# Two token tiles at a time in the fronts of the channel groups, with the ranks found anew (DeltaNet and a low-rank mixer on one core)

## The chip, the core and the metric

One core of a Trainium2 chip. The metric is device time in microseconds (us) of one execution. Engines are named as in the profile: PE is TensorE (PEld its weight loads), DVE is VectorE, ACT is ScalarE, POOL is GpSimd, SP is SyncE, which issues transfers.

## The reference

Two blocks, all in float32. The first runs a delta-rule recurrence over 768 tokens for 4 batches and 8 heads of dimension 48; the second mixes tokens through a rank of 32 and channels through a hidden width of 1536.

```python
k_n = k / (np.linalg.norm(k, axis=-1, keepdims=True) + 1e-06)
for t in range(S):
    y[:, :, t] = einsum('bhd,bhde->bhe', q[:, :, t], state)
    v_old = einsum('bhde,bhd->bhe', state, k_n[:, :, t])
    state = state + beta[:, :, t] * einsum('bhd,bhe->bhde', k_n[:, :, t], v[:, :, t] - v_old)
x = y.transpose(0, 2, 1, 3).reshape(B, S, H * D)      # (4, 768, 384)
h = x.transpose(0, 2, 1) @ U @ V                       # U (768, 32), V (32, 768)
u = x + h.transpose(0, 2, 1)
out = u + np.maximum(u @ w_ch1, 0.0) @ w_ch2           # 384 -> 1536 -> 384
```

## The kernel before

The recurrence is done in chunks of 64 tokens. A batch has 12 chunks; six of them make a unit, so there are 8 units n, two to a batch. Units 0, 2, 4, 6 use the SBUF tile slot_87 and units 1, 3, 5, 7 slot_88, so the loads for a unit wait until the unit two before it is done.

For each unit: `load` brings k, q, v and a second copy of k (called z in the names) in pieces of 72 KB; `grams` transposes k and q on PE (L478), copies them out on ACT (L493) and makes the products of a chunk with itself (L505), which DVE masks (L518, L536); `norms` takes the norms of k from the diagonal, and scales v on DVE (L461). `blocks` inverts the triangular 32x32 blocks on DVE: a transposition into gs (L587), a scaling (L591), pairs of multiply and subtract (L596, L602), a transposition back into zz (L609); then the blocks are joined on PE (L652, L666, L692 to L713). `recur(b)` first lets PE apply the inverse (L811, L822), then goes through the 12 chunks of a batch: PE L860, DVE z (L873), PE L888, DVE s (L898, in the first chunk the copy L900), with the outputs on PE (L775, L789) and copied by ACT into X (L759).

The weights come as float64 and are taken apart and put together as float32 on DVE in five instructions a slice (L989, L995, L1001, L1007, L1017) with one on ACT (L974): U, V, six slices of w1, six of w2. SP issues their transfers (L967).

The mixer works in channel groups of 256 tokens (GT), three to a batch (i = 0, 1, 2). Each has a `front` and a `wide` part. In the front of the first group of a batch PE forms x^T U for the whole batch (L1040) and DVE copies it to tt (L1046). Then a group's two tiles of 128 tokens go through `block(c)`, one tile each: PE multiplies tt with V (L1054) into one PSUM bank, DVE adds it to x in place (L1058), PE transposes the tile in three pieces (L1062), ACT copies them into ut (L1065). `wide` waits for both tiles of the group, then PE does 36 matmuls into the hidden width (L1132), ACT the relu (L1088), DVE sums for a seven-product scheme (L1104, L1111), PE 42 matmuls back (L1169), and DVE adds the products to x (L1117); the result goes out through SP (L1121).

PSUM is split into four pairs of banks; a step that needs PSUM takes a pair, also where it uses one bank of it. Once the last chunks of batch 0 are out, one pair becomes the two banks of the mixer.

The order of all instructions is fixed when the program is built. Every part is a Python generator that yields `op(engine, cost, ...)` for each step; `run()` keeps a clock of assumed costs for each engine and picks, of the steps that can start soon, the one with the lowest rank. A rank is the second argument of `begin`, or, if the part is named in the text PLACES (L140 to L164, 91 entries), the number there. `hold` (L238) says how much later than the earliest a step with a good rank may start. The engines then run their queues in the order so found, each instruction waiting for what it needs. A change of ranks, of an assumed cost or of the engine that a step is booked on can therefore move any instruction on any queue.

In `load`, the second half of the pieces of units 2 to 7 is issued by POOL (L378), but its time is booked on SP.

Of the kernel before, what the change touches and what calls it, by code (L numbers as in the profile page):

```python
# [11 lines left out]
ALU = mybir.AluOpType  # L12
# [7 lines left out]
GT = 256  # L20
# [6 lines left out]
def kernel(  # L27
# [20 lines left out]
    nc = tc.nc  # L48
# [45 lines left out]
    def dve(n):  # L94
        return (n + 151) / 960.0

    def act(n):
        return 0.16 + n / 1200.0
# [39 lines left out]
            waits[i] = s  # L138

    PLACES = """  # L140
    add_up b1 i0 15.701; block b0 i0 c0 64.5; block b0 i1 c2 71.091; block b0 i1 c3 56.313
    block b0 i2 c5 93.473; block b1 i0 c0 14.618; block b1 i0 c1 14.618; block b1 i1 c2 14.618
    block b1 i1 c3 14.618; block b1 i2 c4 14.618; block b1 i2 c5 14.618; block b2 i0 c0 93.5
    block b2 i0 c1 93.5; block b2 i1 c2 93.5; block b2 i1 c3 93.5; block b3 i0 c0 65.835
    block b3 i0 c1 65.835; block b3 i2 c4 65.835; block b3 i2 c5 65.835; blocks n0 1.5
    blocks n3 97.0; blocks n5 79.5; diagonals n1 h0 59.5; front b1 i0 79.5
    front b2 i0 58.8; gather b0 i0 h1 c0 70.591; gather b0 i1 h1 c0 70.591; gather b0 i1 h1 c1 70.591
    gather b1 i0 h1 c1 79.0; gather b1 i2 h1 c0 97.0; gather b2 i0 h0 c0 21.0; gather b2 i1 h1 c0 21.0
    gather b2 i1 h1 c1 21.0; grams n2 i0 81.482; grams n2 i1 89.482; grams n3 i0 20.0
    grams n5 i0 31.5; grams n5 i1 20.5; grams n7 i0 13.5; joins n1 h0 12.5  # L150
    joins n2 h0 -3.0; joins n2 h1 -3.0; joins n7 h0 106.5; joins n7 h1 102.5
    last_sum b0 i0 74.5; last_sum b2 i0 27.644; load n0 namev halves(0, 1) 74.591; load n1 namek halves(0, 1) 49.32
    load n1 nameq halves(0, 1) 49.32; load n1 namez halves(0, 1) 49.82; load n4 namek halves(0, 1) 86.5; load n7 namek halves(0, 1) 75.587
    load_beta u0 14.5; load_weights 68.5; norms n1 59.3; norms n2 81.804
    norms n7 91.523; outputs b0 c2 3.5; outputs b0 c4 76.5; outputs b0 c6 46.644
    outputs b0 c7 36.586; outputs b0 c9 90.5; outputs b1 c11 9.0; outputs b1 c5 57.185
    outputs b2 c0 37.5; outputs b2 c11 37.5; outputs b2 c5 37.5; outputs b3 c5 79.0
    placed n6 i1 j0 6.5; prepare n2 h1 5.0; prepare n3 h1 37.477; products n0 i0 j1 58
    products n0 i1 j1 58; products n1 i0 j0 81.119; products n2 i0 j1 3.5; products n2 i1 j0 76.0
    products n3 i0 j0 66.5; products n3 i0 j1 21.301; products n4 i1 j0 58.0; products n5 i1 j0 79.5  # L160
    products n5 i1 j1 79.5; products n6 i1 j0 53.243; products n6 i1 j1 70.0; products n7 i1 j0 87.58
    recur b2 46.313; recur b3 72.5; relu b0 i1 60.403; relu b1 i2 23.537
    wide b0 i0 81.619; wide b0 i1 92.619; wide b2 i1 103
    """  # L164
    PLACES = dict(x.strip().rsplit(" ", 1) for x in PLACES.replace("\n", ";").split(";") if x.strip())

# [42 lines left out]
    def run():  # L209
        stall = {}  # L210
        while waits or woken:
            while woken:
                i = woken.pop(0)
                at = max([0.0] + [done[x] for x in asked[i]])
                if at > ready[i]:
                    last[i] = None
                advance(i, None, max(at, ready[i]))
            some = {}
            for i, s in waits.items():
                e, was = s["e"], last.get(i)  # L220
                at = max(was[1] if was and was[0] == e else ready[i], clock[e])
                if s["port"]:
                    at = max(at, clock["port"])
                if s["take"]:
                    banks, of = places(s)
                    if not of:
                        continue
                    at = max(at, min(banks[y] for y in of))
                if s["mode"] and s["mode"] != state["mode"]:
                    at += SWITCH  # L230
                stall[i] = late(s, at)[1]
                some.setdefault(e, []).append((at + stall[i], i))
            picks = []
            for e, them in some.items():
                soon = min(at for at, _ in them)
                them.sort(key=lambda x: (not waits[x[1]]["rush"], x[1]))
                for at, i in them:
                    hold = 0.5 if i[0] < 13 else HOLD if i[0] < 90 else SWITCH  # L238
                    if at > soon + hold:
                        continue  # L240
                    if not any(a < at and a + waits[x]["cost"] < at + 0.05 for a, x in them):
                        picks.append((at, i))
                        break
            at, i = min(picks)
            at -= stall[i]
            s, got = waits[i], None
            if s["take"]:
                banks, of = places(s)
                got = min(of, key=lambda y: (banks[y], y))
                del banks[got]  # L250
            if s["e"] == "pe":
                pace(at, at, 0.0)
            cost = cost_of(s)
            if s["e"] == "pe":
                crossed, more = late(s, at)
                state["lot"] += s["words"]
                if state["lot"] > LOT:
                    state["lot"] -= LOT
                    cost += more
                    behind = max(0.0, state["hw"] - crossed - more - 0.5)  # L260
                    state["fetched"] = crossed + more + FETCH + 0.6 * behind
                pace(at, at + cost, s["flow"])
            state["now"] = clock[s["e"]] = at + cost
            if s["port"]:
                clock["port"] = at + cost
            if s["mode"]:
                state["mode"] = s["mode"]
            for tag, x in s["give"]:
                free[tag][x] = state["now"] + s["lat"]
            last[i] = s["e"], state["now"]  # L270
            advance(i, got, state["now"] + s["lat"])
# [4 lines left out]
    def one(x):  # L276
        return P[:, BANK["pair"][x]]
# [86 lines left out]
    def load(n, name, halves):  # L364
# [7 lines left out]
            e = "sp" if halves == (0,) else "act"  # L372
        else:
            e = "sp"
        queue = dict(sp=nc.sync, act=nc.scalar)[e]
        for g in halves:
            if n >= NU and g:
                queue = nc.gpsimd  # L378
            for s in range(1, 4, 2) if name == "z" else range(4):
                to = dict(k=s, q=s, v=s % 2 * 2 + s // 2, z=s // 2)[name]  # L380
                yield op(e, 0.65, port=False)
                queue.dma_start(  # L382
                    out=t[half(1 - g if name == "z" else g), :, to, 0:D],
                    in_=src[b, 4 * g + s, hf * UC * L : (hf + 1) * UC * L, :].rearrange(
                        "(c t) d -> t c d", t=L
                    ),
                )
                after = landing(384)
                if name == "z" or s % 2:
                    emitted((name, n, g, s // 2), after)  # L390
# [165 lines left out]
    def halves(t, split):  # L556

        size = BK // split
        flat = t.rearrange("p a b -> p (a b)")[:, 0 : split * size * (BK + (split > 1))]
        return flat.rearrange("p (u x) -> p u x", u=split)[:, :, 0 : size * BK].rearrange(  # L560
            "p u (a b) -> p u a b", b=BK
        )[:, :, :, 0:size]
# [467 lines left out]
    def front(b, i):  # L1030
# [17 lines left out]
        cs = list(range(i * GT // 128, (i + 1) * GT // 128))  # L1048
        ut = uts[b, i] = mix.tile([128, KT, GT], FP32, name="ut")

        def block(c):
            o = yield op("pe", 0.65, "F", take="pair", words=4)
            p_h = one(o)[:, 0:DM]
            nc.tensor.matmul(  # L1054
                p_h, v_sb[:, c * 128 : (c + 1) * 128], tt, start=True, stop=True
            )
            yield op("dve", dve(384), give=[("pair", o)])
            nc.vector.tensor_tensor(out=x[:, c], in0=x[:, c], in1=p_h, op=ALU.add)  # L1058
            o = yield op("pe", 0.56, "F", take="pair", words=6, flow=0.32)
            p_u = one(o)[:, 0:DM].rearrange("p (t n) -> p t n", t=KT)  # L1060
            for t in range(KT):
                nc.tensor.transpose(p_u[:, t], x[:, c, t * 128 : (t + 1) * 128], ident)  # L1062
            at = c * 128 - i * GT
            yield op("act", act(384), give=[("pair", o)])
            nc.scalar.copy(ut[:, :, at : at + 128], p_u)  # L1065
            emitted(("ut", b, c))

        for c in cs:
            begin(block(c), 2)
        yield need(*[("ut", b, c) for c in cs])  # L1070
        emitted(("front", b, i), 0.1)

    def reserve():
# [157 lines left out]
```

## Time and profile before

| | |
|---|---|
| median of 3 runs | 622.55 us (621.05 to 623.77) |
| the profiled execution's own time | 622.19 us |
| its span, first to last instruction | 620.1 us |
| mean granted PE clock | 0.939 |
| PE busy | 0 to 124 us: 100.1; 124 to 620 us: 489.0 |
| L1132, 864 records | 201.9 us, 385 ns each |
| L1169, 1008 records | 176.1 us, 329 ns each |
| DVE, L596 and L602 | 64.1 and 64.6 us |
| DMA moved | 33.26 MB |

The span is what the profile can divide up; the time of the execution is 2.1 us longer than its span. Granted clock is the share of full TensorE speed that PE was given in a stretch. A float32 matmul shows as two records, a transposition as one. Busy time of an engine is the union of its instructions, so durations of neighbours that overlap add to a little more.

### The profile page before, as it was taken

Reading aid. Unit: us, or ns where it says so; the run is one execution under the profiler, and the core shown is the slowest. Engines: PE = TensorE matmul, PEld = TensorE weight load, DVE = VectorE, ACT = ScalarE, POOL = GpSimd, SP = SyncE. Lnnn points to the kernel's source line nnn. Section 1 sums busy time; section 2 is a strip of 40 time slices with the busy share of each in tenths; the row PEclk is TensorE's granted clock in tenths of the full one; section 3 lists DMA queues with packets and bytes.
Section 4 is the critical chain, followed back from the end, with each engine's and each line's share of the span. In section 5 each row is a group of like instructions: output and inputs, shape, how many; then the busy total and the mean of one; then the engine's idle time right before and its main releaser. Section 6 shows DMA issues by size and latency. Waiting matters only on the chain.

```text
span 620.1 us, 23438 instructions
## 1 busy us (share of the span) xinstructions
PE 589.1 (95%) x10536; PEld 518.6 (84%) x10536; DVE 401.0 (65%) x965; ACT 228.3 (37%) x450; POOL 82.5 (13%) x145
## 2 busy tenths in 40 slices
PE   6678988999999999999999999999999999999997
PEld 5578976789888878799889878889889869898987
DVE  5869997898989613889898128898894123131312
ACT  3465564740342553521621643245324321101020
POOL 3011052410010343200100511401001000000000
PEclk9766565999999999999999999999999999999999
DMA  9840568850000332410000611600000000000000
GB/s 146 159 88 5 177 177 177 186 123 14 15 4 29 64 75 52 77 37 0 30 3 13 113 41 30 133 2 3 30 3 14 16 3 9 18 5 21 15 12 25
DMA packets 72004, 33.26 MB, mean 54 GB/s; under 512 B 59616, under 2 KB 70368, under 8 KB 71904
## 3 DMA queue, kind: packets, MB, share of 16 engines
q1 hardware_dynamic: 66112, 24.98, 18.3%
q0 software_dynamic: 4192, 6.49, 4.6%
q8 instruction: 82, 1.34, 0.9%
q10 hardware_dynamic: 1600, 0.30, 0.3%
q14 instruction: 18, 0.15, 0.1%
HBM read 27.03 MB, written 4.72 MB: 51 GB/s over the span
## 4 chain that ended last, share of the span: by engine, by line
PE 82%; DVE 9%; SPq 5%; issue 2%; DMA 1%; ACT 0%; ACTq 0%; DVEq 0%
PE P L1132 30%; PE P L1169 27%; SPq L382 4%; PE P L505 3%; PE P L478 2%; PE P L860 2%; PE P L1054 2%; PE P L775 2%; PE P L888 2%; PE P L811 2%; PE P L789 2%; DVE prod L596 1%; DVE xt L602 1%; PE P L822 1%; PE P L666 1%
## 5 line engine op out<-in xcount | busy, mean ns | idle before, releaser
L1132 PE MATMUL P<-ut,w_sb 128*128 128x256 f32 x864 | 201.9, 385 | 0.0
L1132 PEld LDWEIGHTS P<-ut,w_sb 128*128 128x128 f32 x864 | 159.4, 190 | 22.4 <-issue 0.6
L1169 PE MATMUL P<-w_sb,hs 128*128 128x192 f32 x720 | 125.6, 329 | 0.0
L1169 PEld LDWEIGHTS P<-w_sb,hs 128*128 128x128 f32 x720 | 117.1, 190 | 3.9 <-issue 1.2
L1088 ACT ACTIVATE hs<-P 128x512 f32<-128x512 f32 x72 | 43.0, 597 | 167.1 <-PE P L1132 163.1
L1117 DVE TENSOR_TENSOR X<-X,P 128x192 f32<-128x192 f32 x84 | 29.4, 350 | 62.7 <-PE P L1169 62.1
L602 DVE TENSOR_TENSOR xt<-xt,prod 128x112 f32<-128x112 f32 (+21 forms) x200 | 64.6, 323 | 6.9
L596 DVE TENSOR_TENSOR prod<-gs,xt 128x112 f32<-128x112 f32 (+21 forms) x200 | 64.1, 321 | 4.8
L759 ACT COPY X<-P 64x192 f32<-64x192 f32 x96 | 30.1, 313 | 71.3 <-PE P L789 54.6
L1169 PE MATMUL P<-w_sb,S 128*128 128x192 f32 x288 | 50.5, 329 | 0.0
L1169 PEld LDWEIGHTS P<-w_sb,S 128*128 128x128 f32 x288 | 46.8, 190 | 0.6
L1104 DVE TENSOR_TENSOR S<-hs 128x384 f32<-128x384 f32 x24 | 13.2, 552 | 52.4 <-ACT hs L1088 52.3
L873 DVE TENSOR_TENSOR z<-slot,P 128x192 f32<-128x192 f32 x44 | 15.5, 352 | 45.6 <-PE P L860 30.8
L478 PE MATMUL P<-ident,slot 128*128 128x128 f32 x192 | 30.4, 309 | 13.4 <-DMA slot<-in_k_dram 11.4
L478 PEld LDWEIGHTS P<-ident,slot 128*128 128x128 f32 x192 | 25.0, 158 | 18.3 <-issue 13.2
L731 ACT COPY slot<-zz 32x384 f32<-32x384 f32 x64 | 32.5, 509 | 12.2 <-DVE zz L609 7.9
L493 ACT COPY slot<-P 128x768 f32<-128x768 f32 x30 | 23.7, 803 | 31.1 <-PE P L478 30.9
L581 POOL MEMSET xt<- 128x1056 f32 x8 | 7.8, 980 | 186.7 <-DVE zz L609 186.7
L505 PE MATMUL P<-slot 48*64 48x64 f32 x1536 | 31.8, 238 | 0.5 <-ACT slot L493 0.2
L505 PEld LDWEIGHTS P<-slot 48*64 48x64 f32 x1536 | 28.7, 150 | 3.9 <-ACT slot L493 2.1
L738 POOL MEMSET slot<- 32x384 f32 x32 | 13.6, 424 | 108.6 <-PE P L695 63.0
L382 POOL DMA_DIRECT2D slot<-in_k_dram x36 | 24.2, 679 | 28.1 <-PE P L888 28.1
(119 smaller groups left out, 780.7 us busy)
## 6 DMA issues: line engine op xcount, KB each, us to landing
out_dram<-X SPq DMA_DIRECT2D x24, 192.0 KB, 1.9
slot<-in_k_dram SPq DMA_DIRECT2D x56, 72.0 KB, 4.0
X<-in_moe_w_ch_dram SPq DMA_DIRECT2D x10, 384.0 KB, 5.5
wide<-in_moe_w_ch_dram SPq DMA_DIRECT2D x10, 384.0 KB, 5.1
slot<-in_q_dram SPq DMA_DIRECT2D x40, 72.0 KB, 3.6
slot<-in_v_dram SPq DMA_DIRECT2D x40, 72.0 KB, 2.7
slot<-in_k_dram POOLq DMA_DIRECT2D x36, 72.0 KB, 3.9
slot<-in_q_dram POOLq DMA_DIRECT2D x24, 72.0 KB, 4.6
```

The lines of the kernel that those rows point to most:

```text
L382: queue.dma_start(out=t[half(1 - g if name == "z" else g), :, to, 0:D], in_=src[b, 4 * g + s, hf * UC * L : (hf + 1) * UC * L, :].rearrang ...
L478: nc.tensor.transpose(p_t[:, c // 3, c % 3], t[:, c, 2 * j : 2 * j + 2].rearrange("p s d -> p (s d)"), ident,)
L493: nc.scalar.copy(to, p_t)
L505: nc.tensor.matmul(p_g[half(g ^ (par * i)), par, c], kq[rows, c, j, 0, half(g)], kq[rows, c, j, i, half(g)], start=True, stop=True,)
L596: nc.vector.tensor_tensor(out=prod, in0=gb[:, :, j : j + 1, j + 1 :].to_broadcast([128, split, m, w]), in1=xb[:, :, 0:m, j : j + 1].to_bro ...
L602: nc.vector.tensor_tensor(out=xb[:, :, 0:m, j + 1 :], in0=xb[:, :, 0:m, j + 1 :], in1=prod, op=ALU.subtract,)
L731: nc.scalar.copy(pg[quarter(i), :, at, :, a : a + BK], cut(zc, h)[quarter(i)].rearrange("p r (c j) t -> p r c j t", j=2),)
L759: nc.scalar.copy(x[half(c % 2), c // 2, 4 * D * g : 4 * D * (g + 1)].rearrange("p (j r d) -> p r j d", r=2, d=D), states(p_y)[half(g)],)
L1088: nc.scalar.activation(hs[:, fs[0] : fs[1] + 1 : fs[1] - fs[0]], p_f, ACTF.Relu)
L1117: nc.vector.tensor_tensor(out=to, in0=to, in1=p, op=ALU.add)
L1132: nc.tensor.matmul(p_f[:, fs.index(f)], w1_sb[:, y, 256 * t + 128 * fs.index(f) :][:, 0:128], ut[:, t], start=(t == 0), stop=(t == KT - 1),)
L1169: nc.tensor.matmul(p_o, a[:, f], w2_sb[:, w, f], start=(first and f == 0), stop=(f == HF - 1), skip_group_check=True,)
```

## The change

Four edits. The front takes both tiles of a group in one step: two matmuls into the two banks of one pair, one DVE sum over 768 columns, six transpositions into one pair, one ACT copy of 768. The generator `block(c)` and its ranks are gone. The time of the loads issued by POOL is booked on POOL. `hold` for ranks under 13 is 0.18, as for all others, where it was 0.5. PLACES is another table, with 51 entries; the ranks which are not named in it fall back to the second argument of `begin`. The line numbers of the profile before shift by 10 behind PLACES and by 14 behind the front.

```diff
@@ -138,29 +138,19 @@
             waits[i] = s
 
     PLACES = """
-    add_up b1 i0 15.701; block b0 i0 c0 64.5; block b0 i1 c2 71.091; block b0 i1 c3 56.313
-    block b0 i2 c5 93.473; block b1 i0 c0 14.618; block b1 i0 c1 14.618; block b1 i1 c2 14.618
...
+    blocks n1 13; blocks n2 92.294; blocks n3 71.768; blocks n7 91.5
+    diagonals n2 h1 76.43; front b1 i0 38.243; grams n7 i0 73.776; joins n0 h0 0.5
+    joins n3 h0 25.362; load n0 namez halves(0, 1) 69.0; load n1 namek halves(0, 1) 68.004; load n1 nameq halves(0, 1) 68.004
...
     """
     PLACES = dict(x.strip().rsplit(" ", 1) for x in PLACES.replace("\n", ";").split(";") if x.strip())
 
@@ -235,7 +225,7 @@
                 soon = min(at for at, _ in them)
                 them.sort(key=lambda x: (not waits[x[1]]["rush"], x[1]))
                 for at, i in them:
-                    hold = 0.5 if i[0] < 13 else HOLD if i[0] < 90 else SWITCH
+                    hold = 0.18 if i[0] < 13 else HOLD if i[0] < 90 else SWITCH
                     if at > soon + hold:
                         continue
                     if not any(a < at and a + waits[x]["cost"] < at + 0.05 for a, x in them):
@@ -372,10 +362,10 @@
             e = "sp" if halves == (0,) else "act"
         else:
             e = "sp"
-        queue = dict(sp=nc.sync, act=nc.scalar)[e]
         for g in halves:
             if n >= NU and g:
-                queue = nc.gpsimd
+                e = "pool"
+            queue = dict(sp=nc.sync, act=nc.scalar, pool=nc.gpsimd)[e]
             for s in range(1, 4, 2) if name == "z" else range(4):
                 to = dict(k=s, q=s, v=s % 2 * 2 + s // 2, z=s // 2)[name]
                 yield op(e, 0.65, port=False)
@@ -1048,26 +1038,22 @@
         cs = list(range(i * GT // 128, (i + 1) * GT // 128))
         ut = uts[b, i] = mix.tile([128, KT, GT], FP32, name="ut")
 
-        def block(c):
-            o = yield op("pe", 0.65, "F", take="pair", words=4)
-            p_h = one(o)[:, 0:DM]
+        at = slice(cs[0], cs[-1] + 1)
+        o = yield op("pe", 1.3, "F", take="pair", words=8)
+        p_h = pair(o)[:, :, 0:DM]
+        for m, c in enumerate(cs):
             nc.tensor.matmul(
-                p_h, v_sb[:, c * 128 : (c + 1) * 128], tt, start=True, stop=True
-            )
-            yield op("dve", dve(384), give=[("pair", o)])
-            nc.vector.tensor_tensor(out=x[:, c], in0=x[:, c], in1=p_h, op=ALU.add)
-            o = yield op("pe", 0.56, "F", take="pair", words=6, flow=0.32)
-            p_u = one(o)[:, 0:DM].rearrange("p (t n) -> p t n", t=KT)
+                p_h[:, m], v_sb[:, c * 128 : (c + 1) * 128], tt, start=True, stop=True
+            )
+        yield op("dve", dve(768), give=[("pair", o)])
+        nc.vector.tensor_tensor(out=x[:, at], in0=x[:, at], in1=p_h, op=ALU.add)
+        o = yield op("pe", 0.84, "F", take="pair", words=12, flow=0.64)
+        p_u = pair(o)[:, :, 0:DM].rearrange("p m (t n) -> p m t n", t=KT)
+        for m, c in enumerate(cs):
             for t in range(KT):
-                nc.tensor.transpose(p_u[:, t], x[:, c, t * 128 : (t + 1) * 128], ident)
-            at = c * 128 - i * GT
-            yield op("act", act(384), give=[("pair", o)])
-            nc.scalar.copy(ut[:, :, at : at + 128], p_u)
-            emitted(("ut", b, c))
-
-        for c in cs:
-            begin(block(c), 2)
-        yield need(*[("ut", b, c) for c in cs])
+                nc.tensor.transpose(p_u[:, m, t], x[:, c, t * 128 : (t + 1) * 128], ident)
+        yield op("act", act(768), give=[("pair", o)])
+        nc.scalar.copy(ut.rearrange("p t (m n) -> p m t n", m=NT), p_u)
         emitted(("front", b, i), 0.1)
 
     def reserve():
```

## The prediction

> **What bounds the kernel now.** I read the busy shares first, then the slices, then the span cut into stages, then what each engine waited for, then the chain that ended last.
>
> ```profile
> PE 589.1 (95%) x10536; PEld 518.6 (84%) x10536; DVE 401.0 (65%) x965; ACT 228.3 (37%) x450; POOL 82.5 (13%) x145
> PE   6678988999999999999999999999999999999997
> DVE  5869997898989613889898128898894123131312
> PEclk9766565999999999999999999999999999999999
> ```
>
> One digit is 15.5 us. From the eighth digit on (about 109 us) PE is busy without a break at full clock, so from there the time is the sum of PE's work. Ahead of it PE has gaps, runs at half clock, and DVE is the fuller engine. The same in stages (columns: stretch, its length, busy time of PE, PEld, DVE, ACT, POOL with instruction counts, granted clock, DMA share, GB/s):
>
> ```profile
> 93.00:108.50 15.50, 12.60 (x320) 10.37 (x322) 12.29 (x22) 7.21 (x15) 3.26 (x5) 0.50 0.89 177
> 108.50:124.00 15.50, 15.41 (x306) 11.13 (x301) 13.68 (x24) 11.55 (x19) 6.58 (x10) 0.97 0.85 185
> 155.00:200.00 45.00, 44.63 (x1165) 38.85 (x1163) 40.44 (x102) 14.80 (x31) 2.62 (x5) 1.00 0.05 17
> ```
>
> So a change to this kernel is worth what it does to the first 162 us, plus what it adds to or takes from PE's work after that; PE's waits after 112 us add up to only 3.1 us in the view of waits. What DVE waited for before 125 us (total, times, longest):
>
> ```profile
> DVE slot L461 <- DMA slot<-in_v_dram: 4.5, 1, 4.5
> ...
> DVE s L898 <- PE P L888: 1.7, 4, 0.7
> DVE zz L670 <- PE P L666: 1.4, 2, 1.1
> ...
> DVE tt L1046 <- PE P L1040: 0.9, 1, 0.9
> ```
>
> The longest is L461, the scaling of v of unit 0, behind a transfer. And the chain that ended last shows where DVE hands over to PE for the last time that matters (start, length, what):
>
> ```profile
> 159.69 2.12 DVE zz L609
> 161.85 1.42 PE P L652 x95
> 163.87 2.79 PE P L1132 x12
> 167.60 1.49 PE P L1132 x6
> ```
>
> DVE's transposition L609 of unit 2 (first unit of the second batch) ends at 161.8 and PE's L652, which reads it, starts at 161.85. PE had just run out of other work, so this is the point at which a later DVE makes the kernel longer one for one.
>
> **The fronts by themselves.** There are 24 tiles, so 24 single sums and copies become 12 of double length.
>
> ```profile
> L1058 DVE TENSOR_TENSOR X<-X,P 128x384 f32<-128x384 f32 x24 | 12.6, 550 | 0.8 <-PE P L1054 0.4
> L1065 ACT COPY ut<-P 128x384 f32<-128x384 f32 x24 | 10.7, 486 | 24.1 <-PE P L1062 17.9 <-DVE X L1117 5.3 <-DVE s L898 1.0
> L1111 DVE TENSOR_TENSOR hs<-hs,S 128x768 f32<-128x768 f32 x12 | 11.4, 949 | 0.0
> L493 ACT COPY slot<-P 128x768 f32<-128x768 f32 x30 | 23.7, 803 | 31.1 <-PE P L478 30.9
> ```
>
> ACT: 24 x 0.486 = 11.7 us becomes 12 x 0.803 = 9.6, saved 2.0. DVE: 24 x 0.550 = 13.2. No row has a sum of 768 that reads PSUM; the bounds are the 768 row that reads SBUF, 0.949, and twice the 384 row, 1.10. I take 0.949, the row of the same length (the 768-element ACT and DVE rows both come out near 1.65 to 1.73 of the 384 ones): 12 x 0.949 = 11.4, saved 1.8; by the other bound nothing. Neither is worth anything to the end: after 112 us PE is the bound, and PE's 24 matmuls and 72 transpositions stay. The price is latency in one front: both sums wait for both matmuls (2 x 0.645, from L1054 x2 in 1.29), then 0.95 DVE, six transpositions 0.78, one copy 0.80, in one line. For all fronts but the first, PE fills this with L1132 and L1169 groups of 1.3 and 1.95 us; without that cover each would cost the 0.95 us sum and the 0.80 us copy. The first front has only L478 groups (0.82 us) to put between, and DVE has three weight conversions (L1007, L1017, L989: 0.95 + 0.96 + 0.56) between the copy of tt and the first sum, so PE stands there for about 1.3 us.
>
> **The order found anew.** This is the larger part. I compared the order of instructions on each engine in the two built programs and priced it with the rows of before.
>
> SP's queue. k of unit 1 (eight issues) loses w1's first two 384 KB issues and z of unit 0 (four) ahead of it. v of unit 0 (eight) moves ahead of the last four of q of unit 1 and of z, v of unit 1 stays behind them all, and w1 goes last. Adding issue times (0.66 to 0.94 us each in the SP row of the timeline) v0 is issued by 27 us instead of 37.5 and lands by about 31, before DVE asks for it (33), so the 4.5 us wait goes. v1 ends at 42 to 43 and, with the 2.5 us between v0's last issue and L461's start, is there at 45.0. But the changed DVE order scales v1 (L461) ahead of unit 1's substitution, so DVE meets this transfer instead. q1's second four issues are about 6 us later, which puts L652 of unit 0 some 1 us later (33 to 34, now 32.8). w1's first slice, issued at 43 instead of 16, is needed only after v_sb is converted (61.6 now): 15 us of cover. POOL's clearing of diag (L549) moves behind six more issues (0.66 each, 4 us); DVE's L587 that reads it is 27 us behind it (86.8, 114.1).
>
> DVE's sum. Adding row durations in order, DVE has 33.4 us of work up to L591 of unit 1 in the old order (it starts at 44.58), and 33.6 us up to L461 of v1 in the new (which I put at 45.0). So the two are level at 45 us: the wait gained is the wait given back. From there to the end of unit 2's L609 the new order has one L587 (1.96, unit 3's), one L461 (1.36) and one L458 (0.20) more, and the sums differ by 0.1: +3.6 us. Groups overlap a little (all rows add to 429, busy is 401.0), so x 0.93 = +3.4 us. Up to the copy of tt the new order also has four more conversion steps and three L518 ahead: +4.2 of row time, 4.0 real. That swallows the 0.9 us which DVE waits there for PE. I keep the other waits for PE in this stretch (6.0 us) as they are; the bounds are all gone or half as much again (-6.0, +3.0).
>
> PE after that. At L652 of unit 2 the new order has done one L1054 (0.65) and three transpositions (0.39) more and three L1132 instructions (1.30) fewer: +0.3 us left to do. Changes between full-array matmuls and the small tiles: 78 excursions behind the first L1132 before, 83 now. One costs 0.19 us: three L1132 alone take 1.49 (row above), in a run 1.30. So +0.95. PE's waits after 112 us (3.1 us) I leave; bounds 0 and twice.
>
> Sum: 3.4 - 0.9 + 0.3 + 0.95 = +3.75 us. Against the profiled execution that is a span of 620.1 + 3.75 = 623.9; that execution took 622.19, 0.36 under the median of 622.55, so I add to the median: 626.3 us.
>
> [...] In the row, PE ran 12.60 of 15.5 us busy at clock 0.50, and 15.41 of 15.5 at 0.97: full clock came with the first gapless stretch, just where the first front stands. [...]
>
> **Rivals.**
> - *No change, 623.3.* PE has enough to do when unit 2 is late: 15 more L1132 stand ahead of L652, and the waits of DVE for PE shrink by the 3.4 - 0.9 that come late. What is left is 0.3 + 0.95, less 0.5 of waits. For it: DVE is idle for 11.8 of the 116.8 us between 45 and 161.8. Against: the chain shows L652 starting 0.05 us after L609.
> - *Faster, 618.8.* k1 lands earlier, so PE's 5.3 us wait for it at 19 to 24 us goes, PE runs ahead, DVE's 6.0 us of waits for PE go, and half of the 3.1 us late waits: 3.75 - 6.0 - 1.5 = -3.75. For it: the largest waits of both engines are waits for transfers that the new SP order brings forward. Against: PE has nothing on the chain there; DVE has.
> - *Much slower, 631.3.* The serial first front keeps PE at half clock until the first L1132. About 5.0 us of full-clock PE work (two L1054 pairs 2.6, six L1062 0.78, two L478 groups 1.64) would take twice as long: 626.3 + 5.0. It decides if PE stands more than about 1.3 us between the first L1054 and the first L1132. Against: L478 groups stand between.
> - *The change does less than it says* is excluded by the built order: 12 sums of 768, 12 copies of 768.
>
> **How the numbers follow.** Forecast, slightly slower, 0.47 (its own range 623.5 to 629.5); no change 0.28; faster 0.14; much slower 0.11. A measurement of this kernel can tell about 0.5% (3.1 us) from no change: 619.4 to 625.7. Slower is 0.42 of the forecast plus 0.11 = 0.53; same is 0.28 plus the forecast's low end 0.05 = 0.33; faster 0.14. The range, 619.5 to 632, leaves out about 0.1 on each side: below it most of the faster case, above it a clock loss together with longer waits.
>
> **What would show it.** Right: L461 of unit 0 without a wait and L461 of unit 1 waiting near 42 to 45 us; the copy of tt near 113 to 114 us (now 109.75); L609 of unit 2 ending near 164 to 165 with a gap on PE ahead of L652; L1132 and L1169 means unchanged at 385 and 329 ns; front sums near 0.95. Wrong: L609 of unit 2 at 162 or earlier, PE idle below 28 us in all (31 now), or clock below 0.9 between 109 and 124 us.

## The result and the profile after

The changed kernel takes 625.07 us (median of 20 runs, 622.57 to 627.41), the kernel before beside it 622.28 us (20 runs, 620.23 to 623.77): a ratio of 1.0046, 95% interval 1.0033 to 1.0059. It is slower by 2.9 us by this ratio (2.8 between the medians); 3.75 us were forecast. The profiled execution of the changed kernel took 624.78 us with a span of 622.2 us, so the two profiles show 2.1 us of the difference.

Line numbers have moved: v's scaling L461 is now L451, the transposition L609 is L599, L652 is L642, the copy of tt L1046 is L1036, L1132 is L1118, L1169 is L1155. The front's sums are L1049, its matmuls L1045, its transpositions L1054.

The busy shares and slices of the changed kernel, from its page:

```profile
PE 586.9 (94%) x10536; PEld 516.5 (83%) x10536; DVE 400.9 (64%) x953; ACT 226.8 (36%) x438; POOL 83.2 (13%) x145
PE   4598867999999999999999999999999999999997
DVE  4979898999898523699898227898985123131312
PEclk9856585799999999999999999999999999999999
```

From the ninth digit on the rows of PE and of its clock are as before. The first three digits of PE only trade work among themselves (6 6 7 before, 4 5 9 now); the loss is in its sixth and seventh (78 to 109 us), 8 8 before and 6 7 now, and in the clock's eighth, 9 before and 7 now. A part of the sixth is the clock and no loss: from 77.5 to 93 us it was 0.88 instead of 0.61, and PE got through 504 matmul records instead of 518. The three stretches that the prediction showed, now (columns as there):

```profile
93.00:108.50 15.50, 11.11 (x292) 9.68 (x296) 12.59 (x21) 6.61 (x12) 0.70 (x2) 0.56 0.92 173
108.50:124.00 15.50, 14.65 (x146) 10.37 (x143) 13.97 (x21) 9.52 (x15) 9.65 (x15) 0.78 1.12 223
155.00:200.00 45.00, 45.00 (x1041) 40.00 (x1040) 40.23 (x110) 14.27 (x30) 2.62 (x5) 1.00 0.05 16
```

From 93 to 108.5 us PE gets through 292 matmul records instead of 320, and the clock that was 0.97 in the second stretch is 0.78. To see what this costs, both spans are cut at the same pieces of work: the start of tt's matmuls (L1040, now L1030), the first matmul of the wide stage (L1132, now L1118), the start of unit 2's L652 (now L642), and PE's last matmul. The kernel before (columns as above):

```profile
0.00:107.15 107.15, 83.35 (x2410) 76.58 (x2414) 87.01 (x207) 58.00 (x115) 21.04 (x42) 0.66 0.61 131
107.15:120.59 13.44, 13.35 (x208) 8.81 (x208) 11.26 (x17) 9.81 (x17) 5.02 (x8) 0.92 0.89 177
120.59:161.85 41.26, 41.20 (x305) 37.22 (x305) 38.09 (x85) 11.61 (x18) 4.19 (x7) 1.00 0.30 76
161.85:616.95 455.10, 451.23 (x7619) 395.96 (x7619) 264.26 (x657) 148.90 (x302) 52.21 (x89) 1.00 0.13 30
```

and the changed kernel:

```profile
0.00:110.97 110.97, 82.41 (x2461) 75.58 (x2461) 90.71 (x213) 59.85 (x118) 19.90 (x40) 0.71 0.60 133
110.97:120.46 9.49, 8.89 (x48) 5.44 (x45) 8.14 (x13) 6.31 (x9) 5.40 (x9) 0.78 1.13 221
120.46:165.01 44.55, 44.37 (x413) 39.57 (x411) 41.77 (x86) 13.25 (x21) 5.91 (x10) 1.00 0.34 62
165.01:618.90 453.89, 451.10 (x7621) 395.88 (x7620) 259.96 (x643) 147.34 (x291) 52.01 (x89) 1.00 0.14 30
```

PE is at tt's matmuls 3.82 us later, wins 3.95 us to the wide stage by leaving small work for later (208 matmul records stood in this stage before, 48 now), pays 3.29 us of that in the next stage, and reaches L642 3.16 us later. After it PE's work is the same (451.10 and 451.23 us) and its idle time 1.08 us less (2.79 against 3.87). So the loss is made ahead of 111 us. The other profiles agree that nothing behind L642 tells the variants of one order apart as long as PE's code isn't moved: from the start of unit 2's L642 to the end of the span it is 457.1 or 457.2 us in the changed kernel, e1_conv, e2_gs3, after_light and after_both (the experiments below).

The chain that ended last in the changed kernel shows what was on the path there (start, length, what):

```profile
93.89 0.45 PE P L850 x16
94.34 0.23 PE P L765 x14
94.57 2.72 issue
97.29 0.24 PE P L765
...
111.04 2.75 PE P L1030 x12
113.81 0.56 DVE tt L1036
114.37 0.88 DVE power L997
115.27 0.97 DVE w_sb L1007
...
116.30 0.44 issue
116.74 0.95 DVE X L1049
```

Two things stand out. PE stops for 2.72 us after 14 of a group of 16 matmuls, waiting for nothing that the profile shows. And behind tt the weight conversions (L997, L1007) hold the chain until the front's sum. On unit 2 the chain no longer passes through DVE at all:

```profile
158.61 6.47 PE P L1118 x30
165.09 1.35 PE P L642 x95
```

L599 ends at 164.28 us, and PE comes to L642 at 165.01 straight from the wide stage.

Executions of one kernel differ by 2 us and more, and each kernel has one profile. So the verdicts below rest on ratios of many runs, and a profile shows only where that one execution lost time.

### The profile page after: what moved, and what is told of

Read it like the earlier page. It is cut to its first block, busy times and chain, and to the rows that moved or that the text cites. A ratio compares the mean times of both kernels' runs of the same rounds, so it can differ in the third digit from the quotient of the medians.

```text
span 622.2 us, 23389 instructions
## 1 busy us (share of the span) xinstructions
PE 586.9 (94%) x10536; PEld 516.5 (83%) x10536; DVE 400.9 (64%) x953; ACT 226.8 (36%) x438; POOL 83.2 (13%) x145
## 4 chain that ended last, share of the span: by engine, by line
PE 79%; DVE 12%; issue 3%; SPq 2%; ACT 2%; DMA 1%; ACTq 0%; DVEq 0%
PE P L1118 29%; PE P L1155 27%; PE P L495 3%; PE P L468 2%; PE P L850 2%; DVE prod L586 2%; DVE xt L592 2%; PE P L765 2%; SPq L372 2%; PE P L1045 2%; PE P L878 2%; PE P L812 2%; PE P L801 2%; PE P L779 1%; PE P L1030 1%
## 5 line engine op out<-in xcount | busy, mean ns | idle before, releaser
L1118 PE MATMUL P<-ut,w_sb 128*128 128x256 f32 x864 | 202.4, 385 | 0.0
L1118 PEld LDWEIGHTS P<-ut,w_sb 128*128 128x128 f32 x864 | 159.2, 190 | 21.9
L1155 PE MATMUL P<-w_sb,hs 128*128 128x192 f32 x720 | 125.4, 329 | 0.0
L1155 PEld LDWEIGHTS P<-w_sb,hs 128*128 128x128 f32 x720 | 117.0, 190 | 4.4 <-issue 1.2
L1155 PE MATMUL P<-w_sb,S 128*128 128x192 f32 x288 | 50.5, 329 | 0.0
L1155 PEld LDWEIGHTS P<-w_sb,S 128*128 128x128 f32 x288 | 46.7, 190 | 0.7
L468 PE MATMUL P<-ident,slot 128*128 128x128 f32 x192 | 31.7, 317 | 14.6 <-issue 6.5
L888 DVE TENSOR_TENSOR s<-s,P 128x192 f32<-128x192 f32 x40 | 14.1, 351 | 27.5 <-PE P L878 26.4
```

Source lines behind the costliest of these rows:

```text
L468: nc.tensor.transpose(p_t[:, c // 3, c % 3], t[:, c, 2 * j : 2 * j + 2].rearrange("p s d -> p (s d)"), ident,)
L1118: nc.tensor.matmul(p_f[:, fs.index(f)], w1_sb[:, y, 256 * t + 128 * fs.index(f) :][:, 0:128], ut[:, t], start=(t == 0), stop=(t == KT - 1),)
L1155: nc.tensor.matmul(p_o, a[:, f], w2_sb[:, w, f], start=(first and f == 0), stop=(f == HF - 1), skip_group_check=True,)
```

## The experiments

Four theories were tested. *Hand-over*, the prediction's: DVE's L599 of unit 2 sets PE one for one. *First front*: DVE's queue ahead of tt and the first front does. *Code position* (called the stall of PE in the first texts): the 2.72 us stop is PE waiting for its own instructions. *Paired front*: the front itself. All kernels keep the order of instructions on every engine as in their parent, except after_blocks.

| kernel | parent | ratio to before | 95% interval |
|---|---|---|---|
| changed kernel | | 1.0046 | 1.0033 to 1.0059 |
| e2_gs3: 1.7 us of DVE less ahead of L599 | changed | 1.0063 | 1.0039 to 1.0086 |
| e1_conv: 4.4 us of DVE less ahead of the first front's sum | changed | 1.0034 | 1.0016 to 1.0053 |
| before_more: 3.8 us of DVE more ahead of tt | before | 1.0058 | 1.0035 to 1.0080 |
| after_shift16 | changed | 1.0168 | 1.0148 to 1.0188 |
| after_shift32 | changed | 1.0228 | 1.0192 to 1.0263 |
| after_shift48 | changed | 1.0166 | 1.0153 to 1.0179 |
| after_shift64 | changed | 1.0075 | 1.0058 to 1.0091 |
| before_shift32 | before | 1.0276 | 1.0256 to 1.0297 |
| after_light: fewer loads at 88 to 100 us | changed | 1.0021 | 0.9998 to 1.0045 |
| before_light: the same | before | 0.9968 | 0.9944 to 0.9992 |
| after_both: e1_conv and after_light | changed | 0.9994 | 0.9974 to 1.0014 |
| after_blocks: one-tile fronts, new ranks | changed | 1.0331 | 1.0302 to 1.0359 |

### Is the hand-over to L642 the place? (e2_gs3)

Unit 3's L577 stands right ahead of unit 2's L599 on DVE. It is cut to its first 32nd (0.22 us instead of 1.96), so unit 3's transposed grams are left out.

```diff
-        nc.vector.transpose(gs[:, 0:BK], diag.rearrange("p q t -> p t q"))
+        m = 1 if n == 3 else BK
+        nc.vector.transpose(gs[:, 0:m], diag.rearrange("p q t -> p t q")[:, 0:m])
```

> The changed kernel in its own order, with the DVE transposition into gs of unit 3 (1.96 us, right ahead of the transposition out of unit 2 that L652 of unit 2 reads) cut to a 32nd; unit 3 comes out wrong. Theory of the prediction (DVE's last transposition of unit 2 makes the kernel longer one for one): the time falls by about 1.8 us, ratio to before 1.0015. Theory 'first front' and theory 'PE stall': PE gets to L652 0.7 us after that transposition anyway, so nothing changes, ratio 1.0045.

Measured: 1.0063, nothing gained; the 1.0015 of the hand-over theory lies below the interval. It falls; PE, not DVE, is late at L642, as the chain above shows.

### DVE ahead of the first front (e1_conv, before_more)

e1_conv cuts two conversion steps of weight slices 8, 9 and 10 to 64 of 768 columns (the rest of those weights is left unconverted). Each step is 0.73 us shorter; five of the six (3.7 us) lie ahead of tt, the last between tt and the front's sum.

```diff
+            m = 64 if i in (8, 9, 10) else n
...
-                out=mant, in0=low, scalar=2.0 ** -32, in1=upper,
+                out=mant[:, 0:m], in0=low[:, 0:m], scalar=2.0 ** -32, in1=upper[:, 0:m],
...
-                out=power, in0=h, scalar=-(1 << 31), in1=power,
+                out=power[:, 0:m], in0=h[:, 0:m], scalar=-(1 << 31), in1=power[:, 0:m],
```

> The changed kernel in its own order, with two of the five DVE steps (the former L1001 and L1007) of weight slices 8, 9 and 10 cut from 768 columns to 64; w2 comes out wrong. That takes 6 x 0.8 = 4.7 us off DVE between about 101 and 125 us, where the first front waits for it. Theory 'DVE's queue ahead of the first front sets PE's start': the second sum of the fronts (now at 121.1 us) comes 2 to 4 us earlier and the time falls by 2 to 3.5 us, ratio to before 0.999 to 1.002. Theory 'PE's stall of 2.7 us at 94.6 us, where it waits for nothing that the profile shows, is what the change costs': the stall lies ahead of the cut, so less than 1 us falls, ratio 1.003 to 1.005. Theory 'the paired front costs it': as before, 1.004 to 1.005.

Measured: 1.0034, 0.7 us better than the changed kernel for 4.4 us less work, and the intervals overlap. In the profiled execution (625.72 us, 2.2 above the median) the wide stage starts at 119.25 us, 1.2 us earlier than in the changed kernel's, and then loses it. DVE, ahead with the conversions, waits for the transfer of the next weight slice; ACT's step of that conversion waits for DVE, the relu stands behind it on ACT, and PE waits for the relu (timelines of DVE and PE: start, length, instruction, idle time before it in brackets). The list of PE's waits (total, times, longest) still has the stop:

```profile
124.68 0.56 DVE L980 TENSOR_SCALAR power<-X 128x768 int32<-128x768 int32 x1 [4.02 <-DMA X<-in_moe_w_ch_dram]
...
122.08 4.05 PE L1119 MATMUL P<-ut,w_sb 128*128 128x256 f32 x18
128.15 4.15 PE L1119 MATMUL P<-ut,w_sb 128*128 128x256 f32 x18 [2.02 <-ACT hs L1075]
```

```profile
PE P L765 <- issue: 2.7, 1, 2.7
```

The opposite edit, on the kernel before, repeats the last conversion step of slice 8 four times.

```diff
+            for _ in range(4 if i == 8 else 0):
+                nc.vector.scalar_tensor_tensor(
+                    out=dst, in0=mant, scalar=2.0 ** -20, in1=power, op0=ALU.mult, op1=ALU.mult
+                )
             emitted(("weights", i), 0.1)
```

> The kernel before, same order and same PE code, with the last step of the conversion of weight slice 8 done five times in place of once: 4 x 0.95 = 3.8 us more on DVE ahead of the copy of tt and the first front. Theory 'first front': PE's start of gapless work comes later by most of it, +1.6 to +3.8 us, ratio 1.0026 to 1.006. Theory 'code position' with slack on DVE (the changed kernel gave only 0.7 us back for 4.4 us less of DVE): +0 to +0.7 us, ratio 0.999 to 1.0015.

Measured: 1.0058, +3.6 us for 3.8 us of added work (2.2 to 5.0 by the interval). So work added to DVE's queue ahead of tt reaches the end. In the timelines of this kernel (an execution of 627.65 us, 2.1 above its median) tt stands at 115.17 us, where it was at 109.75, and PE waits for a z that stands behind the conversions on DVE:

```profile
105.56 3.94 DVE L1021 SCALAR_TENSOR_TENSOR w_sb<-X,power 128x768 f32<-128x768 f32 x4
...
115.17 0.56 DVE L1050 COPY tt<-P 128x384 f32<-128x384 f32 x1 [1.10 <-PE P L1044]
...
110.41 0.68 PE L789 MATMUL P<-z,slot 64*64 64x48 f32 x16 [3.70 <-DVE z L873]
```

Yet taking 4.4 us away from the changed kernel gave 0.7. Something else is late there too: in the execution profiled the transfer of a weight slice, which no run isolates, and PE with its stop.

### What is the stop of 2.72 us? (the shifted kernels)

In the trace, transfers of 16,384 bytes each run on a queue of kind "instruction". In the changed kernel one moves from 94.0 to 95.5 us by the span's clock, about the stop's first microsecond (94.57 to 97.29), while the DMA column of the windows has 1.27 to 1.31 in each 2 us from 92 to 98 us (it adds up the queues, 79.5% and 47.9% for the two largest); PE goes on 1.8 us after its end. The stop falls after the 4,253rd matmul and weight load of the stream; the kernel before has short ones after the 4,254th and 4,509th. That suggests pieces of code with a fixed length, about 255 such records long; the page of either kernel, with 10,536 matmuls, as many weight loads and 82 such transfers, gives 257 to a transfer. To move the code against these limits without touching the order, small matmuls were put ahead of PE's first instruction (with 32 of them the page has 64 matmul and 64 weight-load records more, half a piece):

```diff
+    for _ in range(32):
+        nc.tensor.matmul(P[0:32, 7, 480:496], ident[0:32, 0:32], ident[0:32, 0:16], start=True, stop=True)
     slots = [const.tile([128, 9792]
```

> The changed kernel with 32 tiny matmuls put ahead of everything on PE, in the 5 us in which it waits for the first transfer; they move every later PE instruction by 32 places in the stream of code, and nothing else. Theory 'PE stall at 94.6 us, in the middle of a group of matmuls, is code that comes late': the stall moves or goes, and the time changes by 1 to 3 us either way; if it goes without another one coming, ratio 1.000. Theories 'first front' and 'paired front': no change beyond 0.5 us, ratio 1.004 to 1.006.

Measured: 1.0228, 11.3 us more than the changed kernel's 1.0046. The stop has moved to another group and grown, with others behind it (PE's waits):

```profile
PE P L781 <- issue: 7.5, 2, 4.9
...
PE P L658 <- issue: 1.9, 1, 1.9
...
PE P L1120 <- issue: 1.5, 1, 1.5
```

In its timeline the stop cuts a group ahead of its last matmul; the transfer of the code begins at 94.7 us, 1.9 us after PE has stopped, and is done at 96.2, 1.5 us before PE goes on:

```profile
92.42 0.41 PE L781 MATMUL P<-z,slot 64*64 64x48 f32 x15
97.71 0.23 PE L781 MATMUL P<-z,slot 64*64 64x48 f32 x1 [4.88 <-issue]
```

Is it the place of the code, or the added matmuls? Three more amounts tell.

> As before with 16 small matmuls: every boundary between pieces of PE's code moves by a quarter of a piece. Theory 'code position': the stall of 2.7 us in L765 near 95 us is gone from its place, others come at the new boundaries, and the time is anything from 0.995 to 1.025 of the kernel before, moving with the sum of PE's waits for nothing that the profile shows ahead of 130 us. Rival 'the matmuls themselves': a quarter to a half of what 32 cost, ratio 1.009 to 1.013, with the stall in L765 kept.

> As before with 48 small matmuls, three quarters of a piece. Theory 'code position': stalls at boundaries a quarter of a piece ahead of those of the changed kernel, time 0.995 to 1.025, following the sum of PE's waits for nothing that the profile shows ahead of 130 us. Rival 'the matmuls themselves': 1.025 to 1.035, more than with 32.

> The changed kernel, all instructions in the same order, with 64 small matmuls ahead of PE's first instruction, where PE waits for its first load anyway; they write nothing that is read. With 32 of them the time rose by 10 us (ratio 1.0228) and new stalls stood in the middle of groups. Theory 'code position' (PE's instructions are loaded in pieces of 256, 16 KB each, and PE stands where the next piece comes late; a small float32 matmul is four instructions, so 32 move every boundary by half a piece and 64 by a whole one): boundaries fall on the same instructions as in the changed kernel, ratio 1.003 to 1.008, span 621 to 625, the one large stall again in L765's group near 95 us and about 2 to 3 us long. Rival 'it is the matmuls themselves' (they delay PE's start or disturb the clock): twice the loss of 32, ratio 1.03 to 1.045.

Measured: 1.0168, 1.0166 and 1.0075. The loss doesn't grow with the number added; it is smallest where the shift is a whole piece, and there the long stop is back in the same lines' group (L767, the changed kernel's L765):

```profile
PE P L767 <- issue: 2.5, 1, 2.5
```

The 0.3% by which 64 small matmuls still exceed the changed kernel has a plain candidate: they run until 8.59 us, and PE's first group starts at 10.91 instead of 5.25 us. Sixteen delay it by only 0.55 us (5.80) and yet cost 1.2%. "The matmuls themselves" falls. Counted in the stream as it is then, the added matmuls included, the stops stand within two records of the changed kernel's place: after the 4,255th record with 16, 32, 48 and 64 added, and again one piece further on, after the 4,509th or 4,510th.

The kernel before, moved by half a piece:

> The kernel before, order unchanged, with the same 32 small matmuls ahead of PE's first instruction. Theory 'code position': the kernel before has stalls of 1.0 and 0.3 us only because its boundaries lie well; moved by half a piece it has one or more stalls of 1.5 us or longer ahead of 150 us in the middle of groups, and its time is 1.003 to 1.025. Rival 'only the changed order is open to it' (its loads crowd the queues at other times): 0.998 to 1.002.

Measured: 1.0276, 16.8 us, beyond the range expected. Its unexplained waits are 12.6 us in all (1.3 in the kernel before), 7.7 of them behind 167 us (the expectation had named the time ahead of 150); the largest lines:

```profile
PE P L791 <- issue: 3.0, 3, 1.9
PE P L777 <- issue: 2.5, 1, 2.5
...
PE P L668 <- issue: 1.8, 2, 1.5
PE P L697 <- issue: 1.7, 1, 1.7
```

So both kernels are sensitive to where their code is cut, by 1.2 to 2.8% with a part of a piece added, several times the difference between them. At most ends of pieces no stop shows: the changed kernel has 82 such transfers and, the wait of 6.5 us at 24 to 31 us aside, waits of this kind at four places, 4.0 us in all. The longest stop was 2.72 us there, 3.74 us with 16 added and 4.88 us with 32.

### Is the stop the 2.9 us? (after_light, before_light, after_both)

The loads of k, q and z of unit 2 crowd the DMA engines from 88 to 100 us. They are cut to one of six chunks; the rest of unit 2's k and q stays what the slot held.

```diff
+        m = 1 if n == 2 and name != "v" else UC
...
-                    out=t[half(1 - g if name == "z" else g), :, to, 0:D],
-                    in_=src[b, 4 * g + s, hf * UC * L : (hf + 1) * UC * L, :].rearrange(
+                    out=t[half(1 - g if name == "z" else g), 0:m, to, 0:D],
+                    in_=src[b, 4 * g + s, hf * UC * L : (hf * UC + m) * L, :].rearrange(
```

> The changed kernel, order and code position kept, but the loads of k, q and z of unit 2, which crowd the queues from 88 to 100 us, carry one of their six chunks (so the rest of what is computed from unit 2's k and q comes from older contents). Theory 'code position': the piece of PE's code that comes 2.7 us late near 95 us waits behind these packets; with them gone the wait in L765 is below 1 us and the ratio falls from 1.0046 to between 0.996 and 1.001. Rival 'first front' (DVE's work ahead of the first front sets PE): DVE's queue is untouched, ratio 1.003 to 1.005 even though the stall goes.

> The kernel before with the same loads of unit 2 cut to one chunk of six. Theory 'code position': its pieces of code came 0.5 us late at most there, so it gains less than the changed kernel does, 0 to 1.3 us, ratio 0.998 to 1.000, and the two kernels end within 0.2% of each other. Rival 'the loads themselves' (they delay data, not code): it gains as much as the changed kernel, and the distance of 0.46% between the two stays.

Measured: 1.0021 and 0.9968. The long stop is gone (0.46 us left in its place), so the loads had a part in it. But the gain, 1.6 us, is less than expected, and the kernel before gains 2.0 us by the same cut: the distance between the two stays at about half a per cent. That these loads, by way of the stop, are the difference falls. That late code as such is the difference doesn't fall with it. In the execution profiled the edit didn't take the late code away: two pieces ahead of that place, which had come in time in the changed kernel's, come late now:

```profile
PE P L780 <- issue: 1.5, 1, 1.5
PE P L813 <- issue: 1.4, 1, 1.4
```

All such waits add up to 4.2 us in after_light and to 4.0 in the changed kernel, and PE comes out of the place of the stop at 97.82 us, no earlier than there (97.29). The chain of after_light shows what follows ahead of tt; DVE's conversions, one behind the other:

```profile
101.31 0.48 DVE X L986
101.82 0.96 DVE X L992
102.78 0.87 DVE power L998
103.65 0.10 DVE z L864
103.83 0.96 DVE w_sb L1008
104.81 0.56 DVE power L980
...
113.52 0.56 DVE tt L1037
```

tt is at 113.52 us, hardly earlier than the 113.81 us with the stop. The stretch from the place of the stop to the start of tt's matmuls, with the same work on PE, in the changed kernel, e1_conv and after_light (columns as in the windows above):

```profile
97.29:110.97 13.68, 12.84 (x335) 11.22 (x334) 12.17 (x21) 7.50 (x16) 1.68 (x3) 0.50 0.78 191
99.12:110.58 11.46, 10.52 (x335) 9.03 (x334) 8.60 (x20) 6.94 (x15) 0.86 (x2) 0.70 0.71 175
97.82:111.14 13.32, 10.33 (x335) 9.01 (x334) 12.50 (x22) 7.62 (x16) 1.61 (x3) 0.76 0.32 92
```

In the changed kernel PE (12.84 us at half clock) and DVE (12.17) both fill it nearly. In after_light the clock is higher and PE needs only 10.33 us, but DVE's 12.50 keep the stretch long; in e1_conv, with less on DVE, it is 2.2 us shorter. So here PE and DVE are late side by side. If that decides the time, both edits together must win more than their sum.

> The changed kernel with both edits at once: the conversion steps of weight slices 8, 9 and 10 cut to 64 columns (alone: ratio 1.0034) and unit 2's loads of k, q and z cut to one chunk of six (alone: 1.0021). Theory 'two chains side by side' (ahead of the first front PE is late by its code and DVE by its conversions, each as late as the other, so that taking away one leaves the other): the gains do more than add up, the copy of tt starts at 109 to 111 us, ratio 0.995 to 0.999. Rival 'they are independent': 1.0034 + 1.0021 - 1.0046 = 1.0009, between 1.000 and 1.002. Rival 'the loss sits elsewhere': not below 1.002.

Measured: 0.9994, 95% interval 0.9974 to 1.0014, tt at 111.05 us. The two edits together take back 0.52%, as much as the change had cost; by themselves they took 0.12% and 0.25%, together 0.37%. The point lies on the side of the two chains, but the interval holds the sum of independent gains (1.0009) too, so the interplay is not shown. Nor is it a return to the kernel before by the change's own causes alone, since the cut of loads helps that kernel too: beside before_light (0.9968) after_both is still 0.26% longer, with intervals that overlap.

### The new ranks with the old front (after_blocks)

The changed kernel with the one-tile front of before put back, ranks and all else as in the changed kernel.

```diff
-        o = yield op("pe", 1.3, "F", take="pair", words=8)
...
+        def block(c):
+            o = yield op("pe", 0.65, "F", take="pair", words=4)
...
+        for c in cs:
+            begin(block(c), 2)
+        yield need(*[("ut", b, c) for c in cs])
```

> The new ranks with the old fronts, one tile at a time; up to the first front the order on PE is that of the changed kernel, from there on it is found anew. Theory 'first front' (DVE's queue ahead of it) and theory 'PE stall': the start is the same, so the time stays 1.5 to 4 us over before, ratio 1.003 to 1.006. Theory 'the paired front costs it': the time falls to that of before, ratio 0.999 to 1.001.

Measured: 1.0331, which no theory expected. With another front the same ranks give another order behind it, and PE waits where it didn't:

```profile
PE P L468 <- DMA slot<-in_q_dram: 6.8, 1, 6.8
PE P L468 <- DMA slot<-in_k_dram: 6.7, 2, 5.1
PE P L850 <- DVE slot L526: 6.0, 1, 6.0
```

So this run says nothing about the price of the paired front by itself, only that ranks and fronts can't be taken apart. The old ranks with the paired front were not run.

## Why the prediction was right, and where it was not

- **Size and sign.** +3.75 us were forecast, +2.9 measured. The direction came from DVE's queue, and before_more shows that 3.8 us more of it, ahead of tt in the kernel before, costs 3.6 us. That the change's own 2.9 us come from there is not shown. The sum left the place of PE's code out, and that alone moved the time by 0.3 to 2.8% in the shifted kernels, so that the number came this near is in part luck.
- **Level at 45 us.** Right in kind. v of unit 0 is scaled at 32.75 us without a wait (it waited 4.45), and v of unit 1 meets its transfer instead, at 43.97 us after a wait of 1.09 (45.0 forecast). The end of unit 1's transposition, 60.36 us against 58.41, shows the gain given back.
- **tt at 113 to 114.** Right: 113.81. But "that swallows the 0.9 us which DVE waits there for PE" was wrong: DVE waits 1.18 us for PE's L1030, which is 3.82 us late too. The step priced DVE's queue and left PE as it was. The forecast missed that PE comes late by its own means, the stop of 2.72 us; the trace of before had this resource in view, as three waits for nothing that the profile shows, 1.3 us in all, and no price was put on it.
- **"This is the point at which a later DVE makes the kernel longer one for one."** The step that failed, the place. L599 of unit 2 ends at 164.28 us as forecast (164 to 165), but without the gap on PE ahead of L642, and e2_gs3 won nothing there. The place is the first front, 50 us earlier: what comes late there stays late in the changed kernel, since PE idles only 0.18 us between the start of the wide stage and L642.
- **+2.5 us at L652, then +1.25 us of PE work behind it.** Measured 3.16, and then -1.06: PE's busy time behind L642 is 0.13 us less, so neither the 0.3 us left to do nor the 0.95 us for five more changes of tile size shows there, and idle time falls by 1.08 us. Two errors of opposite sign brought the sum near.
- **The clock.** From 108.5 to 124 us it is 0.78, where 0.97 stood before and below 0.9 had been named as a sign against the forecast. Full clock comes for good 4.3 us after the start of tt's matmuls (0.50 from 110.97 to 115.23 us, 1.00 from there to 200), where it came 2.2 us after it (0.50 from 107.15 to 109.36, 1.00 from there to 200), so about 2 us more of this stage are at half clock. What decides when it comes is not shown by any run. But e1_conv had full clock sooner (its first digit of 9 that lasts is the eighth, the changed kernel's the ninth) and kept all but 0.7 us of its loss, so the clock is not shown to be a cost of its own; nor is it shown to be none, since e1_conv's execution then waited for a transfer. Ahead of the front the half clock is on the path, as it was before the change: 0.50 in the changed kernel from 97.29 to 110.97 us, 0.50 in the kernel before from 95.45 to 107.08.
- **The paired front.** Sums took 0.949 us each, as priced; PE stood 0.60 us in the first front's stage instead of about 1.3. No sign of a price beyond that, but no run isolates it.
- **Still open:** how the 2.9 us divide between DVE's conversions, the late code and the clock. One at a time the edits give back 0.7 us (conversions) and 1.6 us (loads), both with intervals that overlap the changed kernel's, and no run has the changed order with PE's code all in time.

## What to carry to other kernels

Find the last moment at which the bounding engine isn't full yet, and price a change against everything that must meet there: here the slack of DVE and of PE's own code. Delaying and relieving needn't be worth the same: 3.8 us more on DVE cost 3.6 us, 4.4 us less gave back 0.7. And before a half per cent is put down to an edit of a long unrolled program, move the code by a fraction of a piece: if the time changes more than the edit did, the edit isn't what was measured.

## What the runs showed of the hardware

PE stopped in the middle of groups, for 0.3 to 1 us often and for 2 to 5 us at worst (4.88 us with 32 added); the shifted kernels fit the reading that its next instructions came late. The queue of kind "instruction" carried transfers of 16,384 bytes, 82 or 83 in a run, and the stops stand at ends of pieces of about 255 matmul and weight-load records, at nearly the same places of the stream whatever instructions stand there. In the stops of 1 us and more PE went on 1.2 to 1.9 us after the end of the transfer. With 16, 32 and 48 added small matmuls the time rose by 1.2 to 1.8% over the changed kernel, and with 64 by 0.3%.

What makes a piece late is only in part settled. Crowded DMA engines have a share: at the stop of 2.72 us, with a DMA column of 1.27 and more, the transfer took 1.47 us, and with most of unit 2's loads gone it took 0.90 us and the stop was 0.46 us. But they are not needed. In after_light the stop of 1.40 us falls into a stretch with a DMA column of 0.25 (90 to 93 us), and in the shifted kernel before one of 1.50 us, at 169.2 us behind a rush of small matmuls (121 records of them from 168 us on), into one of 0.05 (168 to 170 us).

Summed over the span, PE's waits for nothing that the profile shows were 1.3 us in the kernel before, 4.0 in the changed kernel, 6.7 with 64 added to it, 8.7 with 48, 10.9 with 16 and 12.8 with 32, the order of their times (ratios 1, 1.0046, 1.0075, 1.0166, 1.0168, 1.0228). Where other edits changed DVE's work or the loads as well, the order doesn't hold (e1_conv has 5.5 us at 1.0034). One wait of this kind is left out of these sums, 6.5 us at 24 to 31 us in the changed kernel and in that with 16. It is unlikely to be code, since PE starts the group behind it at 30.9 to 31.4 us in the changed kernel and also with 16, 32 or 64 added; its cause is not settled.
